# Two dense expert layers after block attention: the second expert's input products for two token groups taken in one block of seven products, summed in PSUM

## The chip, the core and the metric

One Trainium2 chip, one of its cores. The metric is device time in microseconds (us) of one execution of the whole program; the median of three runs of the kernel before is 624.28 us.

## The reference

```
a = softmax([banded q.k of the 31 nearest keys, q.max_of_block(k) + log 32])   # 2 batches, 8 heads, 768 tokens, 64 wide
x = (a @ [v, mean_of_block(v)]) laid out as 1536 tokens x 512                   # float32 throughout
g = x @ w_gate            # 512 x 1536
x = (g * sigmoid(g) * (x @ w_val)) @ w_out                                      # 1536 x 512
h = x @ w_in              # 512 x 2048
out = (h * tanh(softplus(h))) @ w_out2                                          # 2048 x 512, "mish"
```

## The kernel before

**Three stages.** The attention fills the first quarter. Its results, split into a rounded part and a rest (`xh`, `xl`, so that a float32 product is three products of a short type), are the tokens x in three groups of 512 (g = 0, 1, 2). Phase 1 is the first expert, phase 2 the second. Work is a list of items `(phase, c, g, ...)`: one chunk of 128 hidden features c for one token group g. An item makes its hidden values (TensorE into banks 4 to 7), passes them through the activation, splits them into `gt` (three buffers in turn) and multiplies them by the chunk's output weights: 12 products of 512 columns into banks 0 to 3 (line 848), where a run of items of one group adds up. At the end of a run VectorE (line 879) or ScalarE (`copy`, line 273) moves the four banks to `pacc` or `kx`; after the last run of phase 1 that sum is the second expert's input.

**The second expert's hidden values** come from a seven-product scheme (two 2 x 2 block matrices multiplied with seven products in place of eight). One side is a pair of chunks, whose weights `weights_pair` turns into seven blocks. The other is one token group, whose left and right halves are its two columns; `second_input` makes seven forms of it. `hidden_pair` runs the seven products of a unit (pair, group), each of 6 matmuls of 256 columns into a bank of its own (line 1031, `PRODUCTS`), and VectorE adds each bank to quarters of two `tmp` tiles (`combine`, line 287). Mish (line 1069) then runs tile by tile. There are 24 units: 8 pairs by 3 groups.

**Weights** arrive as float64 words in a ring of `NRAW` = 4 buffers (`words32`), are turned into float32 by ScalarE and VectorE, and split into `wsl` slots. The fourth buffer of the ring also takes two of the early loads of v (`means_first`).

**The order of each engine** is set before launch: operations are listed with their dependences and due times (`want`), and `Program.order` walks them with costs of its own and gives each engine at each step the ready operation that is due first. Each engine then runs its list strictly in that order. `EARLY` lets a weight load start 40 us ahead of use.

Of the kernel before, what the change touches and what calls it, by code (L numbers as in the profile page):

```python
# [17 lines left out]
P = 128  # L18
# [23 lines left out]
NRAW = 4  # L42
NCV = 2
NG = 3
NTMP = 8
# [148 lines left out]
def tile_kernel(  # L194
# [137 lines left out]
    def means_first():  # L332
        spare = raw[NRAW - 1].bitcast(F32)
# [259 lines left out]
    for ph, sizes in ((1, RANGES1), (2, RANGES2)):  # L593
        for rn, size in enumerate(sizes):
            r0 = sum(sizes[:rn])
            chunks = range(r0, r0 + size)
            back = rn % 2 == (0 if ph == 1 else 1) and rn > 0
# [17 lines left out]

    last_use = {}
    for n, (ph, c, *_rest) in enumerate(items):
        for name in ("g", "v", "o") if ph == 1 else ("i", "p"):
            last_use[name, c] = n
# [12 lines left out]
    def words32(name, c):  # L632
# [8 lines left out]
        more = [("raw", NRAW - 1, h) for h in range(2)] if k == NRAW - 1 else []  # L641
        dma(rw, src, P * 4096, w=[kr, *more], rel=clock["t"] - EARLY, name=f"t{k}")
# [187 lines left out]
    def out_products(n):  # L830
# [10 lines left out]
        for m, both in steps:  # L841
# [76 lines left out]
    def form(g, j, x):  # L918

        if j < 4:  # L920
            a, nm = (xh, "xh") if x == 0 else (xl, "xl")
            ap, k = (lambda: a[g][:, j, :]), [(nm, 2 * g, j), (nm, 2 * g + 1, j)]
        else:
            ap, k = extra((g * 3 + j - 4) * 2 + x)
        return (lambda: ap().rearrange("p (k t) -> p k t", k=2)), k

    def second_input(g, step):
        (up, ku), (down, kd) = parts(g, 0), parts(g, 1)
        b11, b12 = up[:, :, 0:HALF], up[:, :, HALF:]
        b21, b22 = down[:, :, 0:HALF], down[:, :, HALF:]  # L930

        def split(j, a, r):
            (hi, kh), (lo, kl) = form(g, j, 0), form(g, j, 1)
            op("ACT", c_act(512), lambda: nc.scalar.activation(out=hi(), in_=a, func=AF.Copy), r=r, w=kh)
            op(
                "DVE",
                c_dve(512),
# [5 lines left out]
        def minus(out, a, b, r, w):  # L943
            combine(out, a, b, 512, ALU.subtract, r, w, eng="DVE")

        if step == 0:
            split(0, b11, ku)
            minus(b11, b12, b11, [], ku)
            split(3, b11, ku)
            return  # L950
        split(1, b21, kd)
        split(2, b22, kd)
        minus(b12, b22, b12, kd, ku)
        minus(b22, b22, b11, ku, kd)
        minus(b21, b22, b21, [], kd)
        split(4, b12, ku)
        split(5, b21, kd)
        split(6, b22, kd)
# [46 lines left out]
    PRODUCTS = ((0, 0), (3, 6), (1, 1), (5, 4), (6, 3), (4, 2), (2, 5))  # L1005

    def hidden_pair(n):
# [3 lines left out]
        ph, c, g, at, sz = items[n]  # L1011
        h = slot_of["i", c]
        unit = wsl[:, h : h + 7, :].rearrange("p j (x f) -> p j x f", x=2)
        tiles = [5 + (n + i) % 4 for i in range(2)]
        quarter = {}
        for i, name in enumerate(("y0a", "y0b", "y1a", "y1b")):
            at = (i % 2) * HALF
            quarter[name] = (tmp[tiles[i // 2]][:, at : at + HALF], (("tmp", tiles[i // 2]), "y", i % 2))
        free = [("tmp", tiles[0]), ("tmp", tiles[1]), ("kext", 1)] if n < first2 + 4 else []

        def product(i):
            bk = 4 + counts["p"] % 4
            counts["p"] += 1
            a, b = PRODUCTS[i]
            (xhi, kh), (xlo, kl) = form(g, b, 0), form(g, b, 1)

            def products():
                for kk in range(2):
                    hi, lo = (unit[:, a, x, kk * P : (kk + 1) * P] for x in range(2))
                    for m, (w, x) in enumerate(((hi, xhi), (hi, xlo), (lo, xhi))):  # L1030
                        nc.tensor.matmul(  # L1031
                            bank[bk][:, 0:HALF],
                            w,
                            x()[:, kk, :],
                            start=(kk == 0 and m == 0),
                            stop=(kk == 1 and m == 2),
                        )

            op("PE", 720, products, r=[("w", h + a), *kh, *kl], w=[("bank", bk)], want=want(720))
            return bk  # L1040

        def add(out, a, bk, alu=ALU.add):
            (o, ko), (a, ka) = quarter[out], quarter[a]
            combine(o, a, bank[bk][:, 0:HALF], HALF, alu, [("bank", bk), ka], [ko], eng="DVE")
# [90 lines left out]
```

## Time and profile before

| | |
|---|---|
| median of three runs | 624.28 us (624.27 to 624.75) |
| the profiled execution | 624.95 us, of which the span of the core's work is 622.9 us |
| busy time of TensorE, VectorE, ScalarE | 613.2, 425.3, 282.1 us |
| granted TensorE clock over the span | 1.00 |

The profiled execution's time is 2.05 us over its span: work before the first and after the last instruction. Busy time is the union of an engine's instructions; matmuls overlap one another, so the distance between the starts of two of them, not the length of one, is what a matmul costs.

### The profile page before, as it was taken

The numbers are of one execution on the slowest core, as the hardware profiler recorded it, in microseconds if no ns is written. First come the engines' busy times: TensorE is split into PE (matmuls) and PEld (weight loads), VectorE is DVE, ScalarE is ACT, GpSimd is POOL, SyncE is SP. The second block draws the span as 40 slices with busy tenths as digits, with TensorE's granted clock in tenths as the row PEclk, the third lists the DMA queues.
The fourth block names the chain that finished last, engine by engine and source line by source line (L and its number), as shares of the span: only waits on it lengthen the run. The fifth ranks groups of instructions, "written<-read, shape, count | busy, mean of one in ns | idle before, by whom it ended". The sixth has DMA issues, their size and how long they took to land.

```text
span 622.9 us, 10639 instructions
## 1 busy us (share of the span) xinstructions
PE 613.2 (98%) x4096; PEld 530.1 (85%) x4096; DVE 425.3 (68%) x1010; ACT 282.1 (45%) x646; POOL 23.4 (4%) x37
## 2 busy tenths in 40 slices
PE   8999999999999999999999999999999999999997
PEld 6688999888888888888888889998989898989895
DVE  6798679472555584742566999599739985896553
ACT  4687579553322351321243465465433642362321
POOL 3212111000000000000000000000000000000000
PEclk9999999999999999999999999999999999999999
DMA  8989357030221151210020131113301330010111
GB/s 319 294 226 261 102 179 240 2 115 22 80 90 34 34 185 52 71 66 0 1 67 1 69 102 37 65 69 105 98 1 36 113 123 1 30 39 1 69 67 69
DMA packets 34770, 55.05 MB, mean 88 GB/s; under 512 B 8712, under 2 KB 23176, under 8 KB 34720
## 3 DMA queue, kind: packets, MB, share of 16 engines
q1 hardware_dynamic: 34720, 54.38, 27.6%
q8 instruction: 32, 0.52, 0.3%
q14 instruction: 18, 0.15, 0.1%
HBM read 50.98 MB, written 3.15 MB: 87 GB/s over the span
## 4 chain that ended last, share of the span: by engine, by line
PE 92%; DMA 4%; ACT 1%; DVE 1%; SPq 0%; issue 0%; DVEq 0%
PE bank L848 34%; PE bank L748 32%; PE bank L1031 19%; PE bank L799 3%; DMA att<-in_vt_dram 2%; PE bank L549 2%; PE bank L458 2%; PE bank L533 2%; DMA tmps<-in_vt_dram 1%; DMA pacc<-in_kt_dram 1%; ACT att_tmp L496 0%; SPq L268 0%; DVE pacc L879 0%; PE bank L379 0%; DVE kx L287 0%
## 5 line engine op out<-in xcount | busy, mean ns | idle before, releaser
L748 PE MATMUL bank<-xh,wsl 128*128 128x512 f32 (+1 forms) x672 | 203.1, 362 | 0.3 <-DVE tmps L988 0.3
L748 PEld LDWEIGHTS bank<-xh,wsl 128*128 128x128 f32 x672 | 123.3, 188 | 21.3 <-issue 1.7
L848 PE MATMUL bank<-wsl,gt 128*128 128x512 f32 x576 | 135.5, 390 | 0.0
L848 PEld LDWEIGHTS bank<-wsl,gt 128*128 128x128 f32 x576 | 106.5, 188 | 21.0
L748 PE MATMUL bank<-xl,wsl 128*128 128x512 f32 (+1 forms) x336 | 120.6, 359 | 0.5 <-DVE xl L287 0.5
L848 PE MATMUL bank<-gt,wsl 128*128 128x512 f32 x360 | 91.2, 389 | 0.0
L1031 PE MATMUL bank<-xh,wsl 128*128 128x256 f32 x384 | 80.8, 283 | 1.1 <-ACT tmps L273 1.1
L848 PEld LDWEIGHTS bank<-gt,wsl 128*128 128x128 f32 x360 | 67.4, 188 | 13.9
L287 DVE TENSOR_TENSOR tmps<-tmps,bank 128x256 f32<-128x256 f32 x132 | 53.1, 416 | 33.8 <-PE bank L1031 31.8
L273 ACT ACTIVATE wsl<-cva 128x512 fp32r<-128x512 f32 (+1 forms) x84 | 50.7, 608 | 47.3 <-DVE cva L678 12.8
L748 PEld LDWEIGHTS bank<-xl,wsl 128*128 128x128 f32 x336 | 63.3, 188 | 9.8 <-DVE xl L287 0.7
L988 DVE SCALAR_TENSOR_TENSOR tmps<-tmps,bank 128x512 f32<-128x512 f32 (+1 forms) x42 | 25.5, 606 | 65.9 <-ACT tmps L981 65.8
L273 ACT ACTIVATE gt<-tmps 128x512 fp32r<-128x512 f32 (+1 forms) x77 | 45.5, 594 | 48.3 <-DVE tmps L998 47.1
L287 DVE TENSOR_TENSOR gt<-tmps,gt 128x512 fp32r<-128x512 f32 (+1 forms) x78 | 50.3, 647 | 24.8 <-ACT gt L273 20.5
L1031 PEld LDWEIGHTS bank<-xh,wsl 128*128 128x128 f32 x384 | 64.9, 191 | 2.3 <-ACT tmps L273 1.3
L287 DVE TENSOR_TENSOR wsl<-cva,wsl 128x512 fp32r<-128x512 f32 (+1 forms) x84 | 55.3, 662 | 10.3 <-ACT wsl L273 9.9
L981 ACT ACTIVATE tmps<-bank 128x512 f32<-128x512 f32 (+1 forms) x42 | 22.4, 534 | 85.1 <-PE bank L748 85.1
L1031 PE MATMUL bank<-xl,wsl 128*128 128x256 f32 x192 | 54.3, 283 | 0.0
L1031 PE MATMUL bank<-att_late,wsl 128*128 128x256 f32 x320 | 49.3, 283 | 0.0
L651 ACT ACTIVATE cvs<-raw 128x512 f32<-128x512 f32 x68 | 44.7, 666 | 7.2 <-DVE cva L678 3.7
L667 DVE SCALAR_TENSOR_TENSOR cva<-cvs,cva 128x512 uint32<-128x512 uint32 x68 | 46.4, 688 | 1.3
L1069 ACT ACTIVATE tmps<-tmps 128x512 f32<-128x512 f32 x36 | 22.0, 626 | 49.3 <-DVE tmps L287 49.2
(83 smaller groups left out, 679.0 us busy)
## 6 DMA issues: line engine op xcount, KB each, us to landing
raw<-in_w_out_dram SPq DMA_DIRECT2D x28, 512.0 KB, 4.7
raw<-in_w_in_dram SPq DMA_DIRECT2D x16, 512.0 KB, 4.5
raw<-in_w_gate_dram SPq DMA_DIRECT2D x12, 512.0 KB, 5.7
raw<-in_w_val_dram SPq DMA_DIRECT2D x12, 512.0 KB, 6.0
att<-in_vt_dram SPq DMA_DIRECT2D x24, 192.0 KB, 5.7
att<-in_qt_dram SPq DMA_DIRECT2D x24, 128.0 KB, 3.0
out_dram<-pacc SPq DMA_DIRECT2D x8, 256.0 KB, 2.1
pacc<-in_kt_dram SPq DMA_DIRECT2D x4, 400.0 KB
```

The lines of the kernel that those rows point to most:

```text
L273: cost, fn = c_act(n, psum), lambda: nc.scalar.activation(out=dst, in_=src, func=AF.Copy, scale=scale)
L287: op(eng, c_dve(n), lambda: nc.vector.tensor_tensor(out=dst, in0=a, in1=b, op=alu), r=r, w=w)
L458: nc.tensor.matmul(parts_[2 * j + n // 2][q, cols], qb[d, n, :], moving, start=True, stop=True)
L651: lambda: nc.scalar.activation(out=f32(q), in_=f32(high), scale=2.0**-112, **signed),
L667: lambda: nc.vector.scalar_tensor_tensor(out=a, in0=q, scalar=3, in1=a, op0=ALU.logical_shift_left, op1=ALU.bitwise_or),
L748: nc.tensor.matmul(ps, a, x, start=(kk == 0 and m == 0), stop=(kk == KD - 1 and m == 2))
L799: nc.tensor.matmul(bank[bk][:, col : col + HALF], w[:, a, mm], gg[:, x, 0:sz], start=(n in starts and both == 1 and q == 0 and m % 2 == 0) ...
L848: nc.tensor.matmul(bank[m], lhs, rhs, start=(n in starts and both == 1 and q == 0), stop=(n in ends and both == 0),)
L981: lambda: nc.scalar.activation(out=t, in_=gate, func=AF.Tanh, scale=0.5),
L988: lambda: nc.vector.scalar_tensor_tensor(out=t, in0=t, scalar=1.0, in1=gate, op0=ALU.add, op1=ALU.mult),
L1031: nc.tensor.matmul(bank[bk][:, 0:HALF], w, x()[:, kk, :], start=(kk == 0 and m == 0), stop=(kk == 1 and m == 2),)
L1069: op("ACT", c_act(512), lambda: nc.scalar.activation(out=y, in_=y, func=AF.Mish), w=ky)
```

## The change

For token groups 0 and 1 the seven-product block no longer has the two halves of one group as its columns, but the two whole groups. Each product is then 6 matmuls of 512 columns (a wide unit, 8 of them). Group 2 keeps halves of 256 columns (a narrow unit, 8 of them). In both, the sums that were added by VectorE are now partly built up in one bank: a bank holds a partial sum, ScalarE copies it out (`keep`), and the next product goes on adding to the same bank. Three banks serve a unit, three early copies are taken, three additions remain, and mish runs per quarter (twice on a tile, once straight from a bank). The item order of phase 2, the places where units and weights are listed, `NRAW` (4 to 3) and `NTMP` (8 to 10) change with it.

```diff
-NRAW = 4
+NRAW = 3
-NTMP = 8
+NTMP = 10
...
-        bufs = [(tmp[i], ("tmp", i)) for i in (5, 6, 7, 4)] + [
-            (spare[:, h * 512 : (h + 1) * 512], ("raw", NRAW - 1, h)) for h in range(2)
-        ]
+        bufs = [(tmp[i], ("tmp", i)) for i in (5, 6, 7, 4, 8, 9)]
...
+            if ph == 2:
+                wide = [(ph, c, g, 0, GRP) for g in ((1, 0) if rn == 2 else (0, 1)) for c in chunks]
+                last = [(ph, c, NGRP - 1, 0, GRP) for c in chunks]
+                items += last + wide if rn % 2 else wide + last
+                continue
...
-            if m == 1:
-                second_input(g, 0)
-            elif m == 3:
-                second_input(g, 1)
+            if g and m % 2:
+                second_input(g // 2, m // 2)
...
-        def product(i):
-            bk = 4 + counts["p"] % 4
-            counts["p"] += 1
...
-                            bank[bk][:, 0:HALF],
+                            banks[b][:, 0:wide],
...
-                            start=(kk == 0 and m == 0),
+                            start=(start and kk == 0 and m == 0),
...
-        bk = product(0)
-        y, k = quarter["y0a"]
-        copy(y, bank[bk][:, 0:HALF], HALF, True, [("bank", bk)], [k, *free])
-        add("y0b", "y0a", product(1))
-        add("y0a", "y0a", product(2))
-        add("y1a", "y0b", product(3))
-        bk = product(4)
-        add("y1b", "y1a", bk)
-        add("y0b", "y0b", bk)
-        add("y0b", "y0b", product(5))
-        add("y1a", "y1a", product(6), ALU.subtract)
+        product(0, 0, 0, True)
+        product(2, 6, 3, True)
+        keep(0, 0, 0)
+        product(0, 3, 6, False)
+        product(1, 1, 1, True)
+        keep(0, 1, 0)
+        add(0, 0, 1)
+        mish(0, 0)
+        product(0, 5, 4, False)
+        keep(1, 1, 0)
+        add(1, 1, 2)
+        product(0, 2, 5, False)
+        product(2, 4, 2, False)
+        mish(1, 0, banks[0][:, 0:wide], [kb[0]])
+        mish(1, 1)
+        add(0, 1, 2)
+        mish(0, 1)
...
+        def keep(row, col, b):
+            y, k, free = quarter(row, col)
+            copy(y, banks[b][:, 0:wide], wide, True, [kb[b]], [*k, *free])
...
+        def mish(row, col, src=None, r=()):
+            y, k, free = quarter(row, col)
+            src = y if src is None else src
+            op("ACT", c_act(wide), lambda: nc.scalar.activation(out=y, in_=src, func=AF.Mish), r=r, w=[*k, *free])
...
+    def mish_units(n):
+        for j, pair in plan[n]:
+            weights_pair("i", 2 * pair, n + 1)
+            hidden_pair(j, pair)
...
+        mish_units(n)
```

On TensorE, one unit in the middle of phase 2, before: the seven products (the first row of each; `xh1`, `att_late` are forms of group 1, `wsl` the weights) and the first output products behind them.

```order
L1031 MATMUL bank5_66<-xh1_71,wsl_76 128x256 [waits DVE_49]
...
L1031 MATMUL bank6_67<-att_late_2847,wsl_76 128x256 [waits DVE_49]
...
L1031 MATMUL bank7_68<-xh1_71,wsl_76 128x256 [waits DVE_49]
...
L1031 MATMUL bank4_65<-att_late_2847,wsl_76 128x256 [waits DVE_49]
...
L1031 MATMUL bank5_66<-xh1_71,wsl_76 128x256 [waits Activation_49]
...
L1031 MATMUL bank6_67<-xh1_71,wsl_76 128x256 [waits DVE_49]
...
L1031 MATMUL bank7_68<-att_late_2847,wsl_76 128x256 [waits DVE_49]
...
L848 MATMUL bank0_61<-wsl_76,gt1_86 128x512 x2
```

The same engine in the middle of phase 2 of the change, one wide unit (the first row of each product, and the output products among them).

```order
L1071 MATMUL bank6_67<-xh0_70,wsl_76 128x512
...
L1071 MATMUL bank4_65<-xh1_71,wsl_76 128x512
...
L1071 MATMUL bank6_67<-att_late_3009,wsl_76 128x512 [waits Activation_49]
...
L1071 MATMUL bank7_68<-xh0_70,wsl_76 128x512
...
L1071 MATMUL bank6_67<-att_late_3009,wsl_76 128x512 [waits Activation_49]
L1071 MATMUL bank6_67<-att_late_3009,wsl_76 128x512 x5
L869 MATMUL bank0_61<-wsl_76,gt0_84 128x512 x2
L869 MATMUL bank1_62<-wsl_76,gt0_84 128x512 x2
L869 MATMUL bank2_63<-wsl_76,gt0_84 128x512 x2
L1071 MATMUL bank6_67<-att_late_3009,wsl_76 128x512 [waits Activation_49]
...
L1071 MATMUL bank4_65<-xh1_71,wsl_76 128x512 [waits DVE_49]
```

Before, a bank came round again after four products; now bank 6 takes the first, third, fifth and sixth product, and each of the last three waits for ScalarE's copy of the bank. Six output products of an earlier item stand between the fifth and the sixth.

On ScalarE, the first wide unit of phase 2 of the change, where the function table for mish is loaded (`cvs` and `wsl` are steps of the weights; `tmps<-bank4` are the three early copies of the unit).

```order
L273 ACTIVATE tmps_92<-bank4_65 128x512 [waits DVE_49,PE_49]
L273 ACTIVATE wsl_76<-cva0_80 128x2x256 [waits DVE_49]
L672 ACTIVATE cvs0_82<-raw0_77 128x512 [waits DMAHW7_49,Activation_49]
L273 ACTIVATE tmps_92<-bank4_65 128x512 [waits PE_49]
L273 ACTIVATE wsl_76<-cva1_81 128x256 [waits DVE_49]
L672 ACTIVATE cvs1_83<-raw1_78 128x512 [waits DMAHW1_49,Activation_49]
L1093 ACT_TABLE_LOAD
L1093 ACTIVATE tmps_92<-tmps_92 128x512 [waits DVE_49]
L273 ACTIVATE tmps_92<-bank4_65 128x512 [waits PE_49]
```

The same place of ScalarE before: there the table load stands ahead of two whole mish instructions and of the first copy of the second unit.

```order
L934 ACTIVATE xh2_72<-kx_90 128x512 [waits DVE_49] x2
L1069 ACT_TABLE_LOAD
L1069 ACTIVATE kx_90<-kx_90 128x512 [waits DVE_49]
L1069 ACTIVATE tmps_93<-tmps_93 128x512 [waits DVE_49]
L273 ACTIVATE tmps_93<-bank7_68 128x256 [waits PE_49,Activation_49]
```

On TensorE of the change, the border between the last two runs of output products, near the end of the program (group 0's run ends in `gt1`, group 1's begins in `gt2`).

```order
L869 MATMUL bank0_61<-wsl_76,gt1_85 128x512 [waits DVE_49]
L869 MATMUL bank1_62<-wsl_76,gt1_85 128x512
L869 MATMUL bank2_63<-wsl_76,gt1_85 128x512
L869 MATMUL bank3_64<-wsl_76,gt1_85 128x512
L869 MATMUL bank0_61<-wsl_76,gt2_86 128x512 [waits DVE_49,Activation_49]
L869 MATMUL bank0_61<-wsl_76,gt2_86 128x512 x2
L869 MATMUL bank1_62<-wsl_76,gt2_86 128x512 [waits DVE_49]
L869 MATMUL bank1_62<-wsl_76,gt2_86 128x512 x2
```

Before, the seven products of a unit stood between any two runs; here bank 0 is begun again three matmuls after its last one, and VectorE has to have emptied it in between.

## Rows read from the trace of the kernel before

**Rows 1.** Page, busy time of TensorE and ScalarE, share of the span, instructions.
```profile
PE 613.2 (98%) x4096; PEld 530.1 (85%) x4096; DVE 425.3 (68%) x1010; ACT 282.1 (45%) x646; POOL 23.4 (4%) x37
```
**Rows 2.** Chain that ended last, in order of time: start us, length us, what.
```profile
298.03 4.76 PE bank L748 x21
...
355.15 4.76 PE bank L748 x21
...
382.27 5.03 PE bank L1031 x42
387.30 5.47 PE bank L848 x24
392.77 5.03 PE bank L1031 x42
...
602.77 5.03 PE bank L1031 x42
```
**Rows 3.** TensorE's timeline inside one unit: start us, length us, instructions.
```profile
424.82 0.88 PE L1031 MATMUL bank<-att_tmp_late,wsl 128*128 128x256 f32 x6
425.54 0.28 PE L1031 MATMUL bank<-xh,wsl 128*128 128x256 f32 x1
```
**Rows 4.** Waits of TensorE: in total us, times, longest.
```profile
PE bank L533 <- ACT att_tmp L496: 1.3, 1, 1.3
...
PE bank L1031 <- ACT tmps L273: 1.1, 1, 1.1
```
**Rows 5.** Groups by shape: busy us, mean ns of one, idle before.
```profile
L848 PE MATMUL bank<-wsl,gt 128*128 128x512 f32 x576 | 135.5, 390 | 0.0
L1031 PE MATMUL bank<-att_late,wsl 128*128 128x256 f32 x320 | 49.3, 283 | 0.0
L287 DVE TENSOR_TENSOR tmps<-tmps,bank 128x256 f32<-128x256 f32 x132 | 53.1, 416 | 33.8 <-PE bank L1031 31.8
L879 DVE SCALAR_TENSOR_TENSOR pacc<-bank,pacc 128x512 f32<-128x512 f32 x40 | 25.3, 683 | 8.7 <-PE bank L848 8.7
L273 ACT ACTIVATE tmps<-bank 128x256 f32<-128x256 f32 x24 | 9.2, 384 | 40.4 <-PE bank L1031 40.2
L273 ACT ACTIVATE pacc<-bank 128x512 f32<-128x512 f32 x16 | 9.1, 602 | 2.7 <-PE bank L848 1.8 <-PE bank L799 0.9
L651 ACT ACTIVATE cvs<-raw 128x512 f32<-128x512 f32 x68 | 44.7, 666 | 7.2 <-DVE cva L678 3.7 <-DVE cva L667 2.6 <-DMA raw<-in_w_gate_dram 0.7
```
**Rows 6.** TensorE's timeline where phase 2 begins, with its idle time.
```profile
362.47 0.28 PE L1031 MATMUL bank<-xh,wsl 128*128 128x256 f32 x1
...
371.58 0.28 PE L1031 MATMUL bank<-xh,wsl 128*128 128x256 f32 x1
372.93 0.38 PE L1031 MATMUL bank<-xh,wsl 128*128 128x256 f32 x1 [1.07 <-ACT tmps L273]
```
**Rows 7.** ScalarE's timeline at the same place.
```profile
370.16 1.28 ACT L1069 ACT_TABLE_LOAD   x1
371.46 0.63 ACT L1069 ACTIVATE kx<-kx 128x512 f32<-128x512 f32 x1
372.00 0.61 ACT L1069 ACTIVATE tmps<-tmps 128x512 f32<-128x512 f32 x1
372.52 0.36 ACT L273 ACTIVATE tmps<-bank 128x256 f32<-128x256 f32 x1
```
**Rows 8.** From a product's last matmul (TensorE) to the copy that waits for it (ScalarE).
```profile
382.70 0.28 PE L1031 MATMUL bank<-xh,wsl 128*128 128x256 f32 x1
...
383.02 0.39 ACT L273 ACTIVATE tmps<-bank 128x256 f32<-128x256 f32 x1 [0.36 <-PE bank L1031]
```
**Rows 9.** TensorE's idle times in the attention's first weights, timeline.
```profile
25.57 0.39 PE L748 MATMUL bank<-xl,wsl 128*128 128x256 f32 x1 [0.47 <-DVE xl L287]
...
30.90 0.39 PE L748 MATMUL bank<-xh,wsl 128*128 128x256 f32 x1 [0.27 <-DVE tmps L988]
...
41.70 0.62 PE L533 MATMUL bank<-cst,att_tmp 128*120 128x128 f32 x4 [1.27 <-ACT att_tmp L496]
```
**Rows 10.** Stretches: us, then busy us of TensorE, its weight loads, VectorE, ScalarE, POOL, granted clock, DMA share, GB/s.
```profile
30.00:35.00 5.00, 4.73 (x60) 4.19 (x59) 5.00 (x21) 5.00 (x19) 0.82 (x1) 1.00 1.07 292
...
450.00:500.00 50.00, 50.00 (x311) 45.20 (x310) 37.14 (x81) 24.53 (x45) 0.00 (x0) 1.00 0.19 60
```
**Rows 11.** DMA issues of the weights: times, KB each, median us to landing.
```profile
raw<-in_w_out_dram SPq DMA_DIRECT2D x28, 512.0 KB, 4.7
raw<-in_w_in_dram SPq DMA_DIRECT2D x16, 512.0 KB, 4.5
```
**Rows 12.** VectorE's timeline, two sums taken from banks back to back.
```profile
365.26 1.29 DVE L879 SCALAR_TENSOR_TENSOR kx<-bank,kx 128x512 f32<-128x512 f32 x2
```

More of the change, by code (lines that the diff above doesn't have):

```diff
@@ L614, in tile_kernel @@
     starts = {run[0] for run in runs}
+    Y = range(5, NTMP + 1)
+    first2 = next(n for n, it in enumerate(items) if it[0] == 2)
+    plan, y_of, unit_at, waiting = [[] for _ in items], {}, {}, []
+    for n, (ph, c, g, *_rest) in enumerate(items):
+        if ph == 2 and (g // 2, c // 2) not in waiting:
+            waiting.append((g // 2, c // 2))
+    y_free = list(Y)
+    for n in range(first2 - 1, len(items)):
+        while waiting and (need := 2 if waiting[0][0] else 4) <= len(y_free):
+            j, pair = waiting.pop(0)
+            plan[n].append((j, pair))
+            unit_at[j, pair] = n
+            for c in (2 * pair, 2 * pair + 1):
+                for g in (2,) if j else (0, 1):
+                    y_of[c, g] = y_free.pop(0)
+        if n + 1 < len(items):
+            y_free.append(y_of[items[n + 1][1:3]])
     last_use = {}
     for n, (ph, c, *_rest) in enumerate(items):
-        for name in ("g", "v", "o") if ph == 1 else ("i", "p"):
-            last_use[name, c] = n
+        for name, lag in (("g", 0), ("v", 0), ("o", 1)) if ph == 1 else (("p", 2),):
+            last_use[name, c] = n + lag
+    for (j, pair), n in unit_at.items():
+        last_use["i", 2 * pair] = max(last_use.get(("i", 2 * pair), 0), n)
     slot_of, free_at = {}, [-1] * NHS
@@ L640, in words32 @@
             src = src.rearrange("p k f -> p (k f)")
-        more = [("raw", NRAW - 1, h) for h in range(2)] if k == NRAW - 1 else []
-        dma(rw, src, P * 4096, w=[kr, *more], rel=clock["t"] - EARLY, name=f"t{k}")
+        dma(rw, src, P * 4096, w=[kr], rel=clock["t"] - EARLY, name=f"t{k}")
         words = rw.rearrange("p (n two) -> p n two", two=2)
@@ new lines, in second_input, with split @@
+    def second_input(j, step):
+        if j:
+            (up, ku), (down, kd) = parts(2, 0), parts(2, 1)
+            (b11, b12), (b21, b22) = ((a[:, :, 0:HALF], a[:, :, HALF:]) for a in (up, down))
+            k11 = k12 = ku
+            k21 = k22 = kd
+        else:
+            (b11, k11), (b12, k12) = parts(0, 0), parts(1, 0)
+            (b21, k21), (b22, k22) = parts(0, 1), parts(1, 1)
+        size = 2 * WIDTH[j]
+        def split(i, a, r):
+            (hi, kh), (lo, kl) = form(j, i, 0), form(j, i, 1)
+            op("ACT", c_act(size), lambda: nc.scalar.activation(out=hi(), in_=a, func=AF.Copy), r=r, w=kh)
@@ L1002, in silu_item, with hidden_pair, quarter, product @@
         split_g(n, t, [kt_], sz)
[L1005 to L1012, printed above, removed]
+    def hidden_pair(j, pair):
+        h, wide = slot_of["i", 2 * pair], WIDTH[j]
         unit = wsl[:, h : h + 7, :].rearrange("p j (x f) -> p j x f", x=2)
[L1014 to L1019, printed above, removed]
-        def product(i):
-            bk = 4 + counts["p"] % 4
-            counts["p"] += 1
-            a, b = PRODUCTS[i]
-            (xhi, kh), (xlo, kl) = form(g, b, 0), form(g, b, 1)
+        banks = [bank[4 + (counts["p"] + i) % 4] for i in range(3)]
+        kb = [("bank", 4 + (counts["p"] + i) % 4) for i in range(3)]
+        counts["p"] += 3
+        def quarter(row, col):
+            i = y_of[2 * pair + row, 2 if j else col]
+            keys = [(("tmp", i), "y", half) for half in range(2)]
+            free = [("tmp", i)] + [("kext", 1)] * (i == NTMP)
+            if j:
+                return tmp[i][:, col * HALF : (col + 1) * HALF], keys[col : col + 1], free
+            return tmp[i], keys, free
+        def product(b, a, x, start):
+            (xhi, kh), (xlo, kl) = form(j, x, 0), form(j, x, 1)
+            cost = 6 * (120 if j else 227)
@@ L1054, in hidden_pair, with add @@
-        add("y0b", "y0b", bk)
-        add("y0b", "y0b", product(5))
-        add("y1a", "y1a", product(6), ALU.subtract)
-    first2 = next(n for n, it in enumerate(items) if it[0] == 2)
+            op("PE", cost, products, r=[("w", h + a), *kh, *kl], w=[kb[b]], want=want(cost))
+        def keep(row, col, b):
+            y, k, free = quarter(row, col)
+            copy(y, banks[b][:, 0:wide], wide, True, [kb[b]], [*k, *free])
+        def add(row, col, b):
+            y, k, _ = quarter(row, col)
+            combine(y, y, banks[b][:, 0:wide], wide, ALU.add, [kb[b]], k, eng="DVE")
@@ L1067, in mish_item @@
-        i = 5 + n % 4
-        y, ky = tmp[i], [(("tmp", i), "y", half) for half in range(2)]
-        op("ACT", c_act(512), lambda: nc.scalar.activation(out=y, in_=y, func=AF.Mish), w=ky)
-        split_g(n, y, ky, 512)
+        weights("p", c, n)
+        i = y_of[c, g]
+        split_g(n, tmp[i], [(("tmp", i), "y", half) for half in range(2)], 512)
     prev = 0
```

76 lines of the change are left out of this document (36 added, 40 removed).

## Prediction

> **What bounds the kernel now.** I read the page first: TensorE is busy for 613.2 of 622.9 us [rows 1]. Busy time proves little, since matmuls overlap, so I went on to the chain that ended last, in order of time [rows 2], and looked for its rhythm. In phase 1 an item of 36 matmuls of 512 columns starts every 8.16 us: the piece of 298.03 comes again at 355.15, seven items later, 57.12 / 7 / 36 = 0.2267 us a matmul. In phase 2 a unit and its two items, 42 matmuls of 256 columns and 24 of 512, repeat from 382.27 to 602.77 in 21 equal steps of 10.50 us. Nothing but TensorE stands in that stretch of the chain. Inside a unit six matmuls of 256 start within 0.72 us [rows 3], 0.120 us each. So halving the columns saves 0.107 of 0.227 us, not half: there is a fixed part of about 13 ns in each matmul.
>
> The waits come next, because a chain of one engine's work can hide short ones. TensorE has two of over 1 us [rows 4]: one in the attention, and one of 1.07 us where phase 2 begins, at 372.93 [rows 6]. The granted clock is 1.00, the upper of the two levels (2.4 GHz), in the early and the late stretch alike [rows 10]. Phase 2 is bound by TensorE's issue of matmuls, VectorE is busy for 37.1 of 50 us there and ScalarE for 24.5 [rows 10]. What counts is therefore the number of TensorE's matmuls and any wait that it is given.
>
> **The change part by part, by TensorE's time.**
>
> *Fewer, longer matmuls.* The 16 units of groups 0 and 1 become 8 wide ones. The columns are the same; 16 x 42 = 672 matmuls of 256 become 336 of 512. Two narrow units cost 2 x 42 x 0.120 = 10.08 us, a wide one 42 x 0.2267 = 9.52, so 8 x 0.56 = **4.5 us** go. Bounds: with the chain's own 5.03 for a unit and 5.47 / 24 for a long matmul [rows 2] it is 3.9; with 10.50 less 24 x 0.2267, 5.06 for a unit, it is 4.8.
>
> The Trainium skill, page "TensorE: Matmul & The Clock Gate", section "Back-to-back issue gap", speaks against this: it puts the warm gap at N / 2.4 + 2.5 ns, a fixed part of 2.5 ns, and by it the change would save an estimated 0.8 us. The rows say 13 ns, so here page and measurement differ, and the sum goes by the rows.
>
> *Changes of width.* 10.50 us is 0.02 more than 42 x 0.120 + 24 x 0.2267 = 10.48; I put that to the one change of width and back. Before there were 24 of these, after there are about four in each of 8 narrow units, whose products now stand between output products: **+0.2 us** (0 to 0.5).
>
> *VectorE's additions* fall from seven a unit to three. Of 256 columns they take 0.42 us [rows 5]; two of 512 in a row start 0.60 apart [rows 12]. VectorE is not waited for in the steady part of phase 2, so this gain costs and saves nothing: it is hidden behind TensorE's 10.50 us. ScalarE gets three copies a unit in place of one, and mish in quarters: 8 x 7 operations of 512 and 8 x 7 of 256 in place of 24 copies and 48 mish. At 0.5 us (mish instructions start 0.54 apart [rows 7]) and 0.3 us that is some 45 us where there were 33, on an engine busy for half of the time; hidden as well, but for the next point.
>
> *The early copies, a new wait.* A copy takes a bank that the next product of the same bank must add to. Its path: the last matmul lasts 0.39 us and the next product may start 0.227 after its start, so the result is 0.16 us late; ScalarE starts 0.04 after the result (383.02 against 382.70 + 0.28) [rows 8]; the copy of 512 takes 0.60 [rows 5]; TensorE starts 0.05 after a copy's end (372.93 against 372.52 + 0.36) [rows 6, 7]. That is 0.85 us. Between stand a product of 6 x 0.2267 = 1.36 us, for the third copy six output products, 1.36 as well. The slack is 0.5 us, one ScalarE instruction. In a narrow unit the path is 0.16 + 0.04 + 0.38 + 0.05 = 0.63, and the order puts two to six output products (0.45 to 1.36) beside the product of 0.72 or in its place, a slack of 0.3 to 0.8. Waiting behind the blocked product is all of TensorE. I price this at 0 in the steady part, since the copies stand first or second after finished work in ScalarE's list; the bound above is the second rival.
>
> *The beginning of phase 2.* The wait of 1.07 us came from the table load of 1.28 us in front of two mish instructions and the first copy of a unit [rows 6, 7]. It moves to another place: counted from the first product of phase 2, the second early copy ends at 4.9 us (third product done at 4.08 + 0.20, then 0.60). Behind it ScalarE has a weight split of 256 columns (0.4, like a copy of that size), a `cvs` of 0.67 [rows 5], the load of 1.28, a mish of 0.54 and the third copy of 0.60: it ends at 8.4. TensorE reaches the fifth addition to that bank at 5 x 1.36 + 8 output products x 0.227 = 8.6. The wait is gone if nothing is late. What could be late is the `cvs`: with three buffers its load can only start when the block three before has been converted, and it takes 4.5 us [rows 11], so I leave 0.3: **-0.8 us** (-1.07 to +0.5).
>
> *The last border of runs.* Bank 0 is begun again three matmuls, 0.68 us, after its last one. VectorE needs 0.16 + 0.04 + 0.68 + 0.05 = 0.93 [rows 5], so TensorE waits 0.25; the next banks, 0.60 apart [rows 12] against 0.68 and 0.45 of matmuls, just keep up: **+0.25 us** (0 to 0.7). At the other seven borders I counted over 3.5 us of matmuls.
>
> *The ring of three.* The early weights (`t3` and on) change places with loads of q and v. VectorE and ScalarE are full from 30 to 35 us and DMA is at 1.07 [rows 10], and TensorE's idle times of 0.47, 0.27 and 1.27 us lie there [rows 9]. The bytes are the same, the loads that the first item needs come no later, and the order of TensorE is the same again from about 48 us on. After that it is never idle for long, so a shift there reaches the end in full. **0 us**, from -1 (half of those idle times go) to +1.5 (one more wait like the 1.27). Later weights come one in 8 us against 4.7 for a load [rows 11]: hidden.
>
> *The sum*: -4.5 + 0.2 - 0.8 + 0.25 + 0 = -4.85. Against the profiled execution's 624.95 that is 620.1 us. The median of the runs shown is 0.67 lower than that execution, so I take the same difference from 624.28: **619.4 us**.
>
> **The rivals.**
>
> *A. The forecast*, 618.3 to 620.9, chance 0.68.
>
> *B. Copies late in ScalarE's queue.* ScalarE works strictly in order; if two instructions of 0.52 us are ahead of a copy, all of the slack is gone and TensorE stands for about 0.5 us. There are 48 such copies. The Trainium skill, page "PSUM — Partial Sum Buffer", section "Engine vs sequencer instructions", calls these queues strict FIFO; the copy at 372.52, behind a table load and two mish, agrees. For it: every copy now has something behind it that TensorE needs, and in wide units ScalarE also has weights between. Against it: ScalarE is half idle in phase 2. Three to six late copies give 621 to 622.6 (chance 0.12). At ten the gain is eaten, and from twelve on, 12 x 0.52 = 6.2 us, the kernel is slower by over 0.2%: 625.6 and more (chance 0.05). That is the case on the other side.
>
> *C. The change doesn't save what it says.* If a matmul of 512 columns among the pair products cost twice one of 256 less 2.5 ns, 237 ns, only 0.8 us would go, and the time would be 624.28 - 0.8 + 0.2 - 0.8 + 0.25 = 623.1. This is the page's formula as a mechanism. Against it: phase 1 runs such matmuls, of the same types, for 50 us on end at 0.2267. Chance 0.03.
>
> *D. The start pays for the ring.* A weight of the second or third chunk late by one landing makes TensorE wait 1.3 to 2.5 us more between 25 and 48 us: 620.9 to 622. For it: DMA is at its limit there. Against it: the load for gate weights of the second chunk comes earlier in the new order. Chance 0.12.
>
> **How the numbers follow.** Predicted 619.4 us. The range goes from 618.3, the forecast with the start's gain, to 622.0, which takes in D and half of B: about 0.15 is left out above and a little below. A measurement of this kernel tells 0.2%, 1.25 us, from no change, so faster means below 623.0. Faster: A, D, the milder B and half of C, and of these a little for two together, 0.90. Within 0.2%: 0.05, from C and several late copies. Slower: 0.05, the far end of B.
>
> **What would show it.** The saving: phase 2 with products of 512 starting 0.227 us apart, and a unit of 42 of them taking 9.5 us in the chain. If they start 0.237 apart, C. The early copies: TensorE's waits name ScalarE's copy (line 273) on the product line; under 1 us in all if I am right, 2 to 3 for the mild B, 6 for the severe one. The beginning of phase 2: a wait at the fifth product of the first wide unit of 0.3 us or none. The border: some 0.25 us on VectorE's line 900, about 8 us before the last matmul ends. The start: the same steady rhythm of 8.16 us begins at the same time as before within 1 us; if it begins later, D. I would be wrong altogether if the changed kernel's TensorE showed waits of over 5 us in phase 2.

## The result and the profile after

The changed kernel takes 619.04 us, the median of six runs (617.98 to 620.29); the kernel before, on the same chip, 624.19 (623.65 to 624.75). The ratio is 0.9918, 95% interval 0.9903 to 0.9932: 5.1 us less. A second set of runs gave 618.86 against 624.81, ratio 0.9905 (0.9889 to 0.9920). The prediction was 619.4.

The first thing to see is the page of the profile: busy time and instructions, to be held against [rows 1].

```profile
span 617.1 us, 9812 instructions
...
PE 608.6 (99%) x3762; PEld 512.7 (83%) x3762; DVE 391.1 (63%) x879; ACT 295.9 (48%) x679; POOL 23.5 (4%) x37
```

There are 334 recorded matmuls fewer (336 by the code), VectorE has 34 us less and ScalarE 14 us more. Where this comes out is shown by the chain that ended last: start, length, what.

```profile
437.05 6.80 PE bank L1071 x30
443.85 1.36 PE bank L869 x6
445.21 2.72 PE bank L1071 x12
447.93 9.52 PE bank L869 x42
457.45 6.80 PE bank L1071 x30
...
512.53 0.71 PE bank L1071 x6
...
523.04 0.71 PE bank L1071 x6
...
600.87 0.70 DVE pacc L900
601.71 9.61 PE bank L869 x41
611.35 2.05 DVE pacc L900 x3
```

A wide unit is 30 + 12 = 42 matmuls in 6.80 + 2.72 = 9.52 us, with output products between, and comes again after 457.45 - 437.05 = 20.40 us: 90 matmuls at 0.2267 with nothing between. A narrow unit with its two items takes 523.04 - 512.53 = 10.51 us, against 10.50 in [rows 2].

Then TensorE's waits in the whole run: total, times, longest.

```profile
PE bank L261 <- POOL warm L260: 1.1, 1, 1.1
PE bank L546 <- ACT att_tmp L273: 1.0, 2, 0.6
PE bank L455 <- DMA att<-in_qt_dram: 0.9, 1, 0.9
PE bank L530 <- ACT att_tmp L493: 0.5, 1, 0.5
PE bank L769 <- DVE tmps L1028: 0.3, 1, 0.3
PE bank L869 <- DVE pacc L900: 0.2, 1, 0.2
PE bank L530 <- issue: 0.2, 1, 0.2
```

No product (line 1071) waits for a copy. The wait of 1.07 us of [rows 6] is gone; the border of runs is there with 0.2.

Idle time is not all that a wait costs, and the starts of the matmuls show the rest. Here is TensorE at the border:

```profile
597.73 3.79 PE L869 MATMUL bank<-wsl,gt 128*128 128x512 f32 x16
601.71 11.18 PE L869 MATMUL bank<-wsl,gt 128*128 128x512 f32 x48 [0.20 <-DVE pacc L900]
```

The last of the 16 starts at 597.73 + 15 x 0.2267 = 601.13, the next one 0.58 later in place of 0.23, and the one behind that another 0.08 late: by the unrounded starts the border costs 0.44 us. In the kernel before, the wait of [rows 6] cost 1.34 in the same way: 1.35 from 371.58 to 372.93 where 0.12 is the rhythm, and 0.11 on the matmul behind it:

```profile
373.16 0.28 PE L1031 MATMUL bank<-xl,wsl 128*128 128x256 f32 x1
```

ScalarE's timeline at the beginning of phase 2 answers to [rows 7]:

```profile
367.52 0.64 ACT L672 ACTIVATE cvs<-raw 128x512 f32<-128x512 f32 x1
368.18 1.28 ACT L1093 ACT_TABLE_LOAD   x1
369.48 0.63 ACT L1093 ACTIVATE tmps<-tmps 128x512 f32<-128x512 f32 x1
370.01 0.58 ACT L273 ACTIVATE tmps<-bank 128x512 f32<-128x512 f32 x1
```

The third copy ends at 370.59, and in TensorE's timeline the product that adds to its bank starts at 370.76, on the rhythm of the output products ahead of it. The table load is still in the way; it has become short enough, with 0.17 us from the copy's end to the matmul.

**A measure without the start.** The last piece of 21 matmuls of phase 1 [rows 2] starts at 355.15 us in the profile of before and at 354.83 in that of after. The last three additions, the chain's last VectorE piece, start at 611.35 after and before at

```profile
617.16 2.05 DVE pacc L879 x3
```

From the one to the other it is 617.16 - 355.15 = 262.01 us before, and 611.35 - 354.83 = 256.52 after. This stretch holds the end of phase 1 and all of phase 2. Below it is called the stretch; in every kernel whose phase 2 was unaltered it came again to within 0.02 us, so it tells differences that the whole time, which is spread over 2 us, does not.

### The profile page after: what moved, and what is told of

It is laid out like the page before. It is cut to its first block, busy times and chain, and to the rows that moved or that the text cites. A ratio compares the mean times of both kernels' runs of the same rounds, so it can differ in the third digit from the quotient of the medians.

```text
span 617.1 us, 9812 instructions
## 1 busy us (share of the span) xinstructions
PE 608.6 (99%) x3762; PEld 512.7 (83%) x3762; DVE 391.1 (63%) x879; ACT 295.9 (48%) x679; POOL 23.5 (4%) x37
## 4 chain that ended last, share of the span: by engine, by line
PE 92%; DMA 4%; DVE 2%; ACT 1%; issue 0%; SPq 0%; DVEq 0%; ACTq 0%
PE bank L869 34%; PE bank L769 31%; PE bank L1071 19%; PE bank L820 3%; DMA raw<-in_w_gate_dram 3%; PE bank L546 2%; PE bank L455 1%; PE bank L530 1%; DMA pacc<-in_kt_dram 1%; DVE att_tmp L516 1%; DVE att_tmp L476 1%; DVE pacc L900 0%; ACT att_tmp L493 0%; DVE ksm L315 0%; PE bank L376 0%; ACT cvs L672 0%
## 5 line engine op out<-in xcount | busy, mean ns | idle before, releaser
L769 PE MATMUL bank<-xh,wsl 128*128 128x512 f32 (+1 forms) x672 | 202.9, 362 | 0.3 <-DVE tmps L1028 0.3
L769 PEld LDWEIGHTS bank<-xh,wsl 128*128 128x128 f32 x672 | 123.1, 188 | 21.5 <-issue 1.8
L869 PE MATMUL bank<-wsl,gt 128*128 128x512 f32 x576 | 139.1, 390 | 0.2 <-DVE pacc L900 0.2
L273 ACT ACTIVATE gt<-tmps 128x512 fp32r<-128x512 f32 (+1 forms) x81 | 48.2, 596 | 66.4 <-DVE tmps L1038 46.9
L287 DVE TENSOR_TENSOR gt<-tmps,gt 128x512 fp32r<-128x512 f32 (+1 forms) x82 | 53.1, 648 | 33.2 <-ACT gt L273 23.8
L1071 PE MATMUL bank<-xh,wsl 128*128 128x512 f32 (+1 forms) x256 | 70.9, 336 | 0.0
L287 DVE TENSOR_TENSOR wsl<-cva,wsl 128x512 fp32r<-128x512 f32 (+1 forms) x84 | 55.5, 664 | 14.6 <-ACT wsl L273 13.8
L1071 PEld LDWEIGHTS bank<-xh,wsl 128*128 128x128 f32 x256 | 46.1, 189 | 5.6
L287 DVE TENSOR_TENSOR tmps<-tmps,bank 128x512 f32<-128x512 f32 (+1 forms) x38 | 21.2, 558 | 35.7 <-PE bank L1071 26.2
L1071 PE MATMUL bank<-att_late,wsl 128*128 128x512 f32 (+1 forms) x176 | 43.5, 369 | 0.0
L1071 PE MATMUL bank<-xl,wsl 128*128 128x256 f32 (+1 forms) x128 | 43.0, 336 | 0.0
L493 ACT ACTIVATE att_tmp<-att_tmp,st 128x120 f32<-128x120 f32 x96 | 36.8, 386 | 10.3 <-DVE st L476 10.3
```

Of the source, the lines that this page charges most:

```text
L273: cost, fn = c_act(n, psum), lambda: nc.scalar.activation(out=dst, in_=src, func=AF.Copy, scale=scale)
L287: op(eng, c_dve(n), lambda: nc.vector.tensor_tensor(out=dst, in0=a, in1=b, op=alu), r=r, w=w)
L493: lambda n=n: nc.scalar.activation(out=s[:, n, :], in_=s[:, n, :], func=AF.Exp, bias=t[:, 0, n : n + 1], scale=-1.0, accum_out=t[:, 1, n : ...
L769: nc.tensor.matmul(ps, a, x, start=(kk == 0 and m == 0), stop=(kk == KD - 1 and m == 2))
L869: nc.tensor.matmul(bank[m], lhs, rhs, start=(n in starts and both == 1 and q == 0), stop=(n in ends and both == 0),)
L1071: nc.tensor.matmul(banks[b][:, 0:wide], w, v()[:, kk, :], start=(start and kk == 0 and m == 0), stop=(kk == 1 and m == 2), skip_group_chec ...
```

## The experiments

All times are medians; the kernel before on the same chips had 624.7 to 624.8. A ratio is to the kernel before unless it says otherwise.

**The changed kernel again.**

> The changed kernel once more, unaltered, beside the next three. Its six runs lay between 618.0 and 620.3 us, those of the kernel before between 623.7 and 624.8. If the saving is a property of the instruction count, the median is 619.0 again within 0.5 us (ratio 0.992). If the wider spread comes from the start, where weights stand on the chain (a DMA landing 7.4 to 9.3 us long in the chain of the changed kernel), the runs are spread over about 2 us again and the profile differs from the last one only ahead of 50 us. If it was chance, the spread is 1 us like that of the kernel before.

Measured: 618.86 us (617.74 to 620.06), the stretch 611.89 - 355.37 = 256.52 us, the same to the hundredth. The spread is in the start, as the second reading had it; it is not the change's own, since 18 runs of the kernel before beside these lay between 623.72 and 626.16. Nine profiles (this kernel, the changed one and the variants of it below) have the same order of instructions on every engine up to the last item of phase 1. In them the piece of twelve matmuls of phase 1 with which the chain passes 41 to 43 us starts at 40.88, 40.96, 41.53, 41.98, 42.50, 42.51, 43.03, 43.04 and 43.08; the piece at the head of the stretch always follows 312.33 or 312.34 us later. So one profile cannot tell 2 us of the start.

**The width undone.** Each wide matmul of the pair products as two of 256 columns; the order stays. The last pair of lines is in the second form alone; without it part of the left halves' sums is left out.

```diff
-                for kk in range(2):
+                for at, kk in ((at, kk) for at in range(0, wide, HALF) for kk in range(2)):
...
-                            banks[b][:, 0:wide],
+                            banks[b][:, at : at + HALF],
                             w,
-                            v()[:, kk, :],
+                            v()[:, kk, at : at + HALF],
...
-                            start=(start and kk == 0 and m == 0),
+                            start=(start and at == kk == m == 0),
```

> Each pair product of 512 columns is made of two of 256, first the six matmuls of the left half, then the six of the right half, into the same bank; the order on every engine is that of the changed kernel. Theory (a fixed part of 13 ns in each matmul): 336 matmuls more x (2 x 0.120 - 0.2267) = +4.5 us on 619.0, so 623.5, with 623.2 to 624.0; a wide unit takes 10.08 us instead of 9.52. Rival C (a fixed part of 2.5 ns): +0.8 us, 619.9. A third theory, that the gain came from the new order and from the sums in PSUM (fewer waits, less work on VectorE): it stays at 619 and the unit of 84 short matmuls takes 9.5 us.

> The split of the wide products once more, with a bank begun anew only by the left half (in the first form the right half began it anew as well, and the left halves lost part of their sums). The instructions are the same in number, shape and order. Expected: the stretch from the last item of phase 1 to the last addition takes 261.3 us as in the first form, against 256.5 in the changed kernel; the whole 622 to 624 us, depending on the start. If values had any part in the time, the stretch would differ.

Measured: 622.58 us in the first form (ratio 0.9967, 0.9955 to 0.9979), 623.70 in the second (0.9988, 0.9969 to 1.0007). The stretch is 614.58 - 353.29 = 261.29 and 616.13 - 354.85 = 261.28 us: 4.77 and 4.76 more than in the changed kernel. The second form's chain:

```profile
438.24 7.19 PE bank L1071 x60
445.43 1.39 PE bank L869 x6
446.82 2.87 PE bank L1071 x24
449.69 9.55 PE bank L869 x42
459.24 7.19 PE bank L1071 x60
```

A unit is 84 matmuls in 10.06 us now, and 7.19 + 1.39 + 2.87 + 9.55 = 21.00 us come in place of 20.40; 8 x 0.60 = 4.8. Of the 0.60, 0.54 are the matmuls. The other 0.06 are the output products, 1.39 and 9.55 where they took 1.36 and 9.52: behind a piece of short matmuls they take 0.03 us more. TensorE waits nowhere in these units, so the difference is the number of matmuls and their widths. Each matmul has a weight load of its own (3762 of both in the changed kernel, 4098 of both in the first form), and no run tells which of the two the fixed 13 ns belong to. Rival C and the third theory fall. The 2.5 ns of the Trainium skill, page "TensorE: Matmul & The Clock Gate", section "Back-to-back issue gap", which that section gives for a single matmul by itself, would make an estimated 336 x 2.5 ns = 0.8 us; the measurement says 4.77 and decides.

The whole of the first form came out at 622.6, below the expected 623.2; its profiled execution, 622.34, had an early start (40.96).

**The table load moved, in the kernel before and in the changed one.** Behind the last tanh of phase 1:

```diff
-            w=[kt_],
-        )
+            w=[kt_, "tanh"],
+        )
+        if items[n + 1][0] == 2:
+            op(
+                "ACT",
+                0,
+                lambda: nc.scalar.activation(out=warm[:, 0:8], in_=warm[:, 0:8], func=AF.Mish),
+                r=["tanh"],
+                w=["warm"],
+                want=clock["t"] + 3e3,
+            )
```

> The kernel before, with one mish of eight columns of a buffer that nobody needs any more put behind the last tanh of phase 1, so that the table load of 1.28 us happens there; all else in the same order. Theory (the wait of 1.07 us at the beginning of phase 2 came from the table load in front of the first copy): the wait is gone, 624.2 - 1.0 = 623.2 us (623.0 to 623.5). Rival: the copy was late because of the two mish and the weights in front of it, the load only fills time that the engine had anyway: less than 0.3 us, 624.0. Second rival: the load now delays the first part of the output factor of the last item of phase 1, and TensorE waits there instead for up to 1.3 us: 624.2 or more.

> The changed kernel with the mish of eight columns behind the last tanh of phase 1, which took the wait of 1.07 us away in the kernel before (its stretch from the last item of phase 1 to the end went from 262.01 to 260.85 us). Theory (in the changed kernel TensorE reaches the addition behind the table load after the copy has ended, so the load is hidden already): the stretch stays at 256.5 us within 0.1. Rival (the load still costs, spread over later copies): 0.3 to 1.1 us less.

Measured in the kernel before: 623.13 us, ratio 0.9974 (0.9965 to 0.9984). The load is at 358.30, and TensorE's waits have none on the product line:

```profile
PE bank L533 <- DVE att_tmp L519: 1.6, 1, 1.6
PE bank L261 <- POOL warm L260: 1.1, 1, 1.1
PE bank L458 <- DMA att<-in_qt_dram: 1.0, 1, 1.0
PE bank L549 <- ACT att_tmp L273: 0.6, 1, 0.6
PE bank L533 <- issue: 0.2, 1, 0.2
```

The stretch is 615.72 - 354.87 = 260.85, 1.16 less. The wait of [rows 6] was the table load. Of the 1.34 that it cost, 0.18 are still lost with the load moved, in delays of 0.1 us and less at banks that a copy and an addition now free just in time. In the changed kernel the same edit moves the stretch from 256.52 to 609.71 - 353.21 = 256.50: nothing. The load was hidden there, as expected. (Its whole time was 617.65, 617.48 to 617.85, with a start at 40.88; by the stretch that is no gain of the edit. Why all four of its runs were that short stays open.)

**VectorE's additions brought back.** First in the chain of the sums, then beside it:

```diff
-            combine(y, y, banks[b][:, 0:wide], wide, ALU.add, [kb[b]], k, eng="DVE")
+            src = banks[b][:, 0:wide]
...
+                nc.vector.tensor_tensor(out=y, in0=y, in1=src, op=ALU.add)
+                for _ in range(2 if col > row else 1):
+                    nc.vector.scalar_tensor_tensor(
+                        out=y, in0=src, scalar=0.0, in1=y, op0=ALU.mult, op1=ALU.add
+                    )
...
```

```diff
+                for _ in range((1 if j else 2) * (2 if col > row else 1)):
+                    nc.vector.scalar_tensor_tensor(
+                        out=warm, in0=src[:, 0:HALF], scalar=0.0, in1=warm, op0=ALU.mult, op1=ALU.add
+                    )
...
```

> The changed kernel, with VectorE's additions of a unit brought back from three to seven: behind each of them one, or two, that add zero times the bank to the same result, so the values stay. That is 8 x 4 x 0.60 + 8 x 4 x 0.42 = 33 us more on VectorE, all in phase 2, with TensorE's order unchanged. Theory (the fewer additions saved nothing, they are hidden behind TensorE): 619.0 within 0.3 us. Rival (part of the gain came from the relief of VectorE, busy for 65 of 100 us in the steady part now): every unit's last mish comes 1.2 us later and output products wait for it; one wait of 0.3 us in each of 16 units would give 624.

> The changed kernel with the same 33 us of additional VectorE work at the same places as in the run with seven additions a unit (637.0 us, 18 more than the changed kernel), but the added instructions (two of 256 columns for each of 512) write to a buffer that nobody reads, so that the mish behind an addition does not wait for them. Theory 1 (the loss came from the chain: an addition late makes the mish late that stands at the head of ScalarE's queue, behind it the next early copy, behind that TensorE): most of the loss goes, 620 to 625 us. Theory 2 (VectorE itself has become the bound, it has 48.5 of 50 us busy from 350 to 400 us before anything is added): the loss stays, 632 to 638 us, with waits of TensorE on weights and on the output factor.

Measured: 637.04 us (ratio 1.0200, 1.0176 to 1.0224) and 633.79 (1.0141, 1.0121 to 1.0162). The stretch is 274.66 and 271.09: 18.1 and 14.6 us more. VectorE is busy for 426.3 us in both. My theory, 619.0 in the first and 620 to 625 in the second, was wrong in both, and the rival's 624 in the first was far too low as well. The second theory of the second run has the time right, but not the waits: it named weights and the output factor, and TensorE's waits in phase 2, but for the border's 0.2, are for banks of the pair products.

```profile
PE bank L1071 <- DVE warm L1093: 5.9, 7, 2.0
PE bank L1071 <- ACT kx L273: 1.5, 1, 1.5
PE bank L1071 <- ACT tmps L273: 1.3, 2, 1.1
```

Line 1093 is the added work. It reads the bank, so it both fills VectorE and holds the bank until it is done. Three stretches of the second run show where this counts (us, then busy us of TensorE, weight loads, VectorE, ScalarE, POOL, granted clock, DMA):

```profile
370.00:390.00 20.00, 17.94 (x81) 14.24 (x80) 19.69 (x39) 11.96 (x22) 0.00 (x0) 1.00 0.03 3
390.00:410.00 20.00, 16.82 (x86) 13.93 (x85) 19.14 (x41) 12.78 (x27) 0.00 (x0) 0.91 0.30 102
...
490.00:510.00 20.00, 20.00 (x90) 16.54 (x89) 13.08 (x24) 7.60 (x13) 0.00 (x0) 1.00 0.22 77
```

and the same of the changed kernel:

```profile
370.00:390.00 20.00, 20.00 (x93) 16.57 (x92) 19.67 (x35) 14.13 (x28) 0.00 (x0) 1.00 0.15 53
390.00:410.00 20.00, 20.00 (x128) 18.09 (x127) 18.45 (x39) 15.59 (x35) 0.00 (x0) 1.00 0.33 106
...
490.00:510.00 20.00, 20.00 (x90) 16.57 (x89) 10.70 (x17) 9.49 (x17) 0.00 (x0) 1.00 0.26 79
```

From 350 to 410 us the changed kernel's VectorE is busy for 57.05 of 60 us already (weights, splits of the second input and units fall together), and TensorE is just not waiting:

```profile
350.00:410.00 60.00, 60.00 (x307) 51.23 (x306) 57.05 (x107) 41.26 (x80) 0.00 (x0) 1.00 0.28 88
```

What is added there comes late and TensorE pays for it. In the even run of wide units the same additions, holding banks in the same way, cost nothing, so it takes a crowded VectorE for them to cost anything. What they would cost there if they read no bank was not run. The chain of the second run has there

```profile
490.64 6.80 PE bank L1071 x30
497.44 1.36 PE bank L869 x6
498.80 2.72 PE bank L1071 x12
501.52 9.52 PE bank L869 x42
511.04 4.08 PE bank L1071 x18
```

with 20.40 us from one wide unit to the next, as without them. By pieces of the chain that answer to each other (427.50 in the changed kernel to 437.79 here, less 0.59 of later start), 9.7 of the 14.6 us are lost before 437 us; the other 4.9 in two more crowded places, about 455 to 481 and 531 to 556. The chain through mish and ScalarE's queue, on which I had put the loss, is worth about the difference of the two runs, 18.1 - 14.6 = 3.5 us, as far as they can be compared: their added instructions differ in length and number.

Part of the loss is the clock: from 390 to 410 the granted clock is 0.91, so for a part of it TensorE had the lower level (1.2 GHz) after it had been idle for 2.06 of the 20 us ahead and while it was idle for 3.18 more; 17 output products took 4.92 us at 403.40 where 3.88 is the full-clock time of 17 in the chain of the changed kernel.

```profile
401.87 1.53 PE bank L1071 x6
403.40 4.92 PE bank L869 x17
```

**The slack of the early copies.** Each copy of a wide unit twice, and in a second kernel three times, as one entry of ScalarE's list:

```diff
-            copy(y, banks[b][:, 0:wide], wide, True, [kb[b]], [*k, *free])
+            def copies(times=1 if j else 2):
+                for _ in range(times):
+                    nc.scalar.activation(out=y, in_=banks[b][:, 0:wide], func=AF.Copy)
+
+            op("ACT", c_act(wide, True), copies, r=[kb[b]], w=[*k, *free])
```

> The changed kernel with each early copy of a wide unit made twice, one behind the other, in the same place of ScalarE's list (24 more copies of 512 columns, 0.56 us each). Theory (0.5 us of slack at each copy): the path is 0.85 + 0.56 = 1.41 us against 1.36, so 24 x 0.05 = 1.2 us: 620.2, from 619 to 622. Rival (no slack, every copy stands on TensorE's path): 24 x 0.56 = 13.4 us, 632. Second rival (the copies are hidden behind more than one product): 619.0.

> The same with each early copy of a wide unit made three times. Theory (0.5 us of slack): the path is 0.85 + 2 x 0.56 = 1.97 us against 1.36, so TensorE stands 0.6 us at each of 24 copies, +14.6 us: 633.5, from 631 to 637. No slack: 24 x 1.12 = 26.9, 646. Hidden: 619.

Measured: 624.88 us (ratio 1.0008, 0.9993 to 1.0022) and 639.92 (1.0244, 1.0221 to 1.0267). The stretch is 617.01 - 354.32 = 262.69 and 631.98 - 355.36 = 276.62: 6.17 and 20.10 more, on the average 0.26 and 0.84 us for each of the 24 copies. Both times lie above the ranges that I had given. From two to three it is 13.93 / 24 = 0.58, all of a copy. The average hides the beginning of phase 2: with two copies one of them cost 1.0 us there and four of the 24 nothing, while those of the even units cost 0.2 to 0.3 each. So there is slack, and it is smaller than 0.5: one more copy lengthens the path by 0.63 (1.23 for two, 0.60 for one) and loses 0.26, which leaves 0.37. Why, the weight loads show. In the changed kernel the first copy of the unit at 580.95 starts at 582.51 and ends at 583.11; the third product adds to its bank:

```profile
583.45 0.87 PEld L1071 LDWEIGHTS bank<-att_late,wsl 128*128 128x128 f32 x4
```

Its matmul starts at 583.67, but its weights are loaded from 583.45 on, under the matmul before. With two copies, from 587.44 to 588.67, the same place reads (weight loads, then TensorE):

```profile
588.72 1.23 PEld L1071 LDWEIGHTS bank<-att_late,wsl 128*128 128x128 f32 x6 [0.38 <-ACT kx L1086]
```
```profile
588.72 1.66 PE L1071 MATMUL bank<-att_late,wsl 128*128 128x512 f32 x6
590.22 0.39 PE L1071 MATMUL bank<-xh,wsl 128*128 128x512 f32 x1
```

The weight load waits as well. It comes 0.05 us after the copy and is no longer hidden: from 588.72 to the next product's 590.22 the six matmuls take 1.50 us instead of 1.36. A wait of 0.12 us on the rhythm (588.72 against 588.60, the last start at 588.37 and 0.227) so costs 0.26. The Trainium skill, page "TensorE: Matmul & The Clock Gate", section "Step-by-step: what each phase is for", says that the queue can take weight loads ahead of matmuls in flight; the trace agrees, by 0.22 us here, and shows that the load of a matmul which waits is not taken ahead.

**The ring and the tiles alone**, in the kernel before:

```diff
-NRAW = 4
+NRAW = 3
...
-NTMP = 8
+NTMP = 10
...
-        spare = raw[NRAW - 1].bitcast(F32)
-        bufs = [(tmp[i], ("tmp", i)) for i in (5, 6, 7, 4)] + [
-            (spare[:, h * 512 : (h + 1) * 512], ("raw", NRAW - 1, h)) for h in range(2)
-        ]
+        bufs = [(tmp[i], ("tmp", i)) for i in (5, 6, 7, 4, 8, 9)]
...
-        more = [("raw", NRAW - 1, h) for h in range(2)] if k == NRAW - 1 else []
-        dma(rw, src, P * 4096, w=[kr, *more], rel=clock["t"] - EARLY, name=f"t{k}")
+        dma(rw, src, P * 4096, w=[kr], rel=clock["t"] - EARLY, name=f"t{k}")
```

> The kernel before with only the change of buffers: a ring of three raw weights in place of four, ten tiles in place of eight, the mean loads in tiles. Nothing of phase 2's products is changed. Theory (the ring costs nothing, the start changes by some 0.3 us): within 0.6 us of the kernel before on the same chip, and the steady rhythm of phase 1 begins within 1 us of before. Rival D: 1.3 to 2.5 us slower. The other side: up to 1 us faster, if half of the idle time between 25 and 48 us goes.

Measured: 623.62 us, ratio 0.9983 (0.9971 to 0.9995): 0.3 to 1.8 us faster, more than the 0.6 that I had expected and about the 1 us of the other side. The head of the stretch is at 353.84 against 355.15, the stretch is 615.85 - 353.84 = 262.01, to the hundredth that of before. Rival D falls; the ring is hidden from there on, and its start is rather better than worse. How much of that the changed kernel, with another order in its start, keeps, can't be read from starts that vary by 2.2 us.

## Why the prediction was right

The mechanism was right: TensorE's issue of matmuls is the bound, and a long matmul costs less than two short ones. By steps:

*Fewer, longer matmuls* with *changes of width*: -4.5 + 0.2 = -4.3 forecast. The stretch became 5.49 us shorter; with the wait of the table load (1.34) taken off and the border (0.44) put back, -4.59 is left for the two. The first is 8 x (10.06 - 9.52) = -4.3 by the split, near enough to -4.5. The second is then -0.3 in place of +0.2: its sign was wrong. I had counted every change of width at 0.02 and found more of them after than before. But the 0.03 us show where six output products or more stand behind the short matmuls, as they did in the 16 units that are gone. In a narrow unit the short matmuls now stand in four pieces, three of them with two to four output products behind, and unit and items take 10.51 us where 42 x 0.1198 + 24 x 0.2267 = 10.47: 0.04 for all four. Undoing the width gave back more than 4.3, namely 4.77, because the split puts two changes of 0.03 into each wide unit.

*The beginning of phase 2*: -0.8 forecast, with 0.3 left for a late `cvs`. Nothing was left; the `cvs` at 367.52 came in time, and the third copy ended 0.17 us ahead of TensorE, where the prediction had 0.2. The wait was worth more than the prediction had for it: 1.34 by the starts and not its idle 1.07, which was the far end of the range.

*The last border*: +0.25 forecast; TensorE is idle for 0.20 and loses 0.44. The prediction, here as at the beginning of phase 2, took the idle time of a wait for its cost.

*The early copies* at 0: right in the time, but the slack was 0.37 and not 0.5. I counted up to the matmul, and up to it there is 0.51 (583.67 - 583.11 - 0.05); but its weight load waits too, and that costs 0.14 at once. Rival B did not come, with less to spare than I said.

*VectorE's additions*, "costs and saves nothing: it is hidden behind TensorE's 10.50 us": right for the change as made, and the weakest sentence of the argument. I had read VectorE's load from 450 to 500 us [rows 10] and called it the steady part. At the beginning of phase 2 VectorE is full, before (from 370 to 390 us 19.20 of 20) and after. The sums in PSUM are not a by-work there: with as much added work on the banks as seven additions a unit would be, the kernel in this order takes 634 to 637 us and is slower than before. So the width saves, and the fewer additions keep VectorE from taking it back. How much wide products without the sums in PSUM would lose, with a bank of its own for each product as before, is not shown: the added instructions also hold three banks longer.

```profile
370.00:390.00 20.00, 18.93 (x123) 17.15 (x123) 19.20 (x41) 13.01 (x24) 0.00 (x0) 1.00 0.14 40
```

*The ring of three*: 0 forecast; by itself, in the kernel before, it gave 0.3 to 1.8 us. By the medians less the stretch's 5.49, the start of the changed kernel was 0.3 us later on the first chip (-5.15 in all) and 0.5 earlier on the second (-5.95). What sets the start's spread stays open: the order is the same in all nine profiles and the kernel before is spread as widely, so it is not the change's doing, but which landing or which copy decides was not tried.

The sum of the steps, -4.85, was 0.64 short of the stretch's -5.49: changes of width and the beginning of phase 2 gave half a microsecond more each than forecast, the long matmuls and the border 0.2 less each. Of the time of the first set the sum was 0.3 off, as its start gave a part back; that it came so close is in part luck.

## What to carry to other kernels

When TensorE's issue is the bound, count matmuls before columns, and take the price of one from the period of whole units in the chain, changes of width included. Before calling an engine's work hidden, look at its busy time in the most crowded stretch, not the even one: the same additions cost nothing at 490 us and 9.7 of 14.6 us before 437. Where a bank is handed from an engine back to TensorE, the deadline lies ahead of the waiting matmul, because its weight load waits with it; here the slack ended 0.14 us sooner for that. Price a wait by the starts of the matmuls around it, not by the idle time. And where runs differ by more than the effect, compare a stretch of the chain that has the start left out.

## What the runs showed of the hardware

- From the end of the start on, the program repeats to 0.02 us over some 570 us of chain (stretches 256.50 to 256.52, 261.28 and 261.29, 262.01 twice; 312.33 or 312.34 ahead of them); all of the spread of about 2 us is in the first 43.
- A matmul that waits 0.12 us for a bank loses 0.26, since its weight load waits too and is then exposed. Idle times of 0.20 and 1.07 us cost 0.44 and 1.34 in the same way.
- Six and more matmuls of 512 columns behind a piece of 256 take 0.03 us more in all (1.39 and 9.55 against 1.36 and 9.52); in a narrow unit, with two to four behind most pieces, four changes and back cost 0.04 together.
- The table load of 1.28 us is followed by the first mish after 0.02 (368.18 + 1.28 to 369.48), with nothing in between.
